# Transfers of an attention and FFN kernel entered in one list, paced by TensorE's columns, with reads of turned weights ahead of writes

## The chip, the cores and the metric

The kernel runs on one core of one Trainium2 chip. A core has TensorE (PE; its weight loads are PEld in the profile), VectorE (DVE), ScalarE (ACT), GpSimd (POOL) and SyncE (SP). In this kernel SP issues nearly every transfer (DMA); 16 DMA engines carry them. The metric is device time in microseconds of one execution.

## The reference, cut to what matters

Attention with a threshold, for 8 batches of 8 heads of 576 rows by 64, and then a bilinear FFN on 4608 rows of 512. All is float32.

```python
scores = scale * np.matmul(q, k.transpose(0, 1, 3, 2))
thresh = np.max(scores, axis=-1, keepdims=True) - tau
scores = np.where(scores >= thresh, scores, -1000000000.0)
attn = np.exp(scores - np.max(scores, axis=-1, keepdims=True))
attn = attn / (np.sum(attn, axis=-1, keepdims=True) + 1e-09)
x = bridge(np.matmul(attn, v))        # (B,H,S,D) -> (B*S, H*D)
return (x @ w_a) * (x @ w_b) @ w_out  # d_model 512, d_ff 1536
```

## The kernel before

Two heads are handled together, a pair; there are 32 pairs, four to a batch. A pair's 576 query rows are cut into four units of 128 rows and a tail of 64 (u = 0 to 3 and NT = 4), which makes 160 units. The main loop has one slot for each unit, and three more (PV_LAG). A slot g does the first steps of unit g and later steps of the units before it, and fills TensorE's time with pieces of the FFN of rows already finished. The order of work on every engine, SP included, is the order in which the loop writes it: `keep_order` ties each instruction to the one before it on its engine. TensorE's order is planned in columns: `advance` draws matmuls of the FFN from a generator until the columns owed in this slot are used up.

The path of a unit:

- Slot g: TensorE computes its scores (L352), 576 columns of them; VectorE takes the maxima (L359); ScalarE the exponentials into the tile `tw` (L380); VectorE cuts at the threshold and sums (L383), and takes the reciprocal (L396); ScalarE normalises (L402).
- Slot g + 1, `turn_blocks`: VectorE transposes `tw` in blocks of 32 by 32 (L446), and SP writes it to a scratch buffer in DRAM, `swap`, by four transfers of 144 KB (72 KB for a tail; L457). `tw` has three buffers.
- Slot g + 2, `turn_back`: SP reads `swap` back in another order, into the tile `wT` (L466: one transfer of 576 KB; L469: two of 144 KB for a tail). By these two transfers the weights are turned. `wT` has two buffers.
- Slot g + 3, after 65% of the slot's share of FFN work, if the unit ends a part: `weighted` multiplies the weights by v (L483), and ScalarE and VectorE take the product out of PSUM (L490, L491). A part is units 0 and 1, or units 2, 3 and the tail. The first batch has other parts, and its first eight units are turned on TensorE and not through DRAM.

Within a slot SP's order is: the four writes of the unit before (`turn_blocks`), behind VectorE's transposes; then the read of the unit before that (`turn_back`, after `weighted` when there is one in the slot, since it needs the buffer of `wT` that `weighted` frees); at the end the loads of q (L147, three slots ahead of use), of k (L147, four ahead) and of v (L170), and the outputs that were pending when the slot began (`store`, L833). q and k are transposed by VectorE (`prep`, L320) one or two slots ahead of their scores. In a later batch the first eight slots hold units 0 and 1 of its four pairs, the next twelve units 2, 3 and the tail.

The FFN's first two matrices are L633 (products of a fast scheme with seven multiplications, 128 columns each) and L706, the last L763 (256 columns). Its results go through tiles `kept` of the tag `osb` (four buffers, shared with `u`, L663) to the output.

Of the kernel before, what the change touches and what calls it, by code (L numbers as in the profile page):

```python
# [22 lines left out]
PV_LAG = 3  # L23
# [7 lines left out]
ROOM = 1024  # L31
PORTIONS = (0.3, 0.35, 0.15, 0.2)
# [20 lines left out]
def kernel(  # L53
# [69 lines left out]
    scratch = pool("scratch", 3, space=bass.MemoryType.DRAM)  # L123
# [11 lines left out]
    def load(i, name, engine=nc.sync):  # L135

        b, hp = pairs[i]
        src = {"q": q, "k": k}[name[0]]
        n0, n1 = {"k": (0, NB), "q0": (0, HALF // Q), "q1": (HALF // Q, NB)}[name]
        bufs = HP if name == "k" else Q_BUFS  # L140
        most = NB if name == "k" else NB - HALF // Q
        t = work.tile([P, most, Q], FP32, tag=name[0] + "T", bufs=bufs, name=name[0] + "T")[:, 0:n1 - n0]
        for j in range(2):
            rows = src[b, 2 * hp + j].rearrange("(e n) d -> e n d" if name == "k" else "(n e) d -> e n d", e=Q)
            for h in range(2):
                r = slice((2 * j + h) * Q, (2 * j + h + 1) * Q)
                engine.dma_start(t[r], rows[:, n0:n1, h * Q:(h + 1) * Q])  # L147
        loaded.setdefault(i, {})[name] = t
# [9 lines left out]
    def load_v(i, again=False):  # L158
# [3 lines left out]
        for j in range(2):  # L162
            rows, half = v[b, 2 * hp + j], loaded[i]["v"][j * D:(j + 1) * D]
            if i >= HP or again:
                if i < HP:
                    rows = rows.rearrange("(c s p) d -> p c s d", c=2, p=Q)
                else:
                    rows = rows.rearrange("(p c s) d -> p c s d", c=2, p=Q)
                for c in range(2):
                    nc.sync.dma_start(half[c * Q:(c + 1) * Q], rows[:, c])  # L170
            else:
                nc.sync.dma_start(half, rows.rearrange("(s p) d -> p s d", p=D))
# [21 lines left out]
    for F in range(NF):  # L194
# [4 lines left out]
             "layer": False, "reading": False, "first": 0}  # L199
# [117 lines left out]
    def prep(i, name):  # L317

        mT = loaded[i].pop(name).rearrange("p n e -> p (n e)")
# [121 lines left out]
    def turn_blocks(i, u):  # L441
# [10 lines left out]
        for g in range(G):  # L452
            if u < NT:
                to, n = swap[g], G
            else:
                to, n = swap[g % 2, (1 - g // 2) * D:(2 - g // 2) * D], 2
            nc.sync.dma_start(to.rearrange("(r p) e -> p r e", p=Q),  # L457
                              t[g * Q:(g + 1) * Q, 0:n * NSLOT].rearrange("p (r s) e -> p r (s e)", r=n))

    def turn_back(i, u):  # L460

        swap = swaps.pop((i, u)).rearrange("g p e -> p g e")
        if u < NT or i < HP:
            turned[i, u] = turned_tile()
            n = G if u < NT else 2
            nc.sync.dma_start(turned[i, u][:, 0:n].rearrange("p g s e -> p g (s e)"), swap)  # L466
        else:
            for y in range(2):
                nc.sync.dma_start(turned[i, 2 + y][:, G].rearrange("p s e -> p (s e)"), swap[:, y])  # L469
# [69 lines left out]
    def weighted(i, h):  # L539

        b, hp = pairs[i]
        n = width(i, h)
# [287 lines left out]
    def store(n):  # L830

        for _ in range(n):
            nc.sync.dma_start(*pending.pop(0))  # L833
# [7 lines left out]
    running = {"ffn": None, "owed": 0.0, "left": 0, "done": 0, "rest": 0, "room": 0}  # L841

    def advance(cols):
        running["owed"] += cols
        while running["owed"] > 0:
# [19 lines left out]
            else:  # L865
                running["owed"] -= step
                running["left"] -= step
                running["done"] = running["done"] + step if rest else 0
# [56 lines left out]
    for g in range(len(units) + PV_LAG):  # L925
        written = len(pending)
        state["converted"] = state["added"]
        here = g < len(units)
        converting = bool(early.get(g)) or bool(early.get(g - 1))
        if here:  # L930
            i, u = units[g]
            scores(i, u)
        exchange_blocks()
# [33 lines left out]
        if g > BY_PE:  # L967
            advance(PORTIONS[1] * pace)
            n = g - PV_LAG
            if BY_PE <= n < len(units) and part(*units[n]):  # L970
# [4 lines left out]
                weighted(*part(*units[n]))  # L975
                running["owed"] -= NSLOT * width(*part(*units[n])) // 2
            if BY_PE + 1 < g <= len(units) + 1:
# [43 lines left out]
    state["over"] = True  # L1021
    while complete or blocks or running["ffn"] is not None:
# [35 lines left out]
```

## Time and profile before

| what | us |
|---|---|
| median of 3 runs | 1463.66 (1454.89 to 1464.56) |
| the profiled execution | 1467.37 |
| its span, first to last instruction | 1465.6 |
| TensorE busy | 1387.9 |
| VectorE busy | 1014.9 |
| ScalarE busy | 682.9 |
| GpSimd busy | 479.5 |

The granted clock of TensorE was 0.994 of full speed on average. The transfers moved 223.21 MB, 152 GB/s over the span; packets of the queue on which SP issues took 60.7% of the time of the 16 DMA engines.

In the profile's lines the letter L is followed by the line in the kernel; "out<-in" names what an instruction writes and reads. SPq stands for SP's queue, whose instructions only issue transfers and wait. A row of waits gives who waited, for whom, the sum in us, how many times, and the longest. "Issue" as a releaser means that the engine waited for nothing that the profile shows. A row of issued transfers ends in the size of one and the median time from issue to landing. A line of a timeline starts with the start in us, and how long. [...]

### The profile page before, as it was taken

The numbers are of one execution on the slowest core, as the hardware profiler recorded it, in microseconds if no ns is written. First come the engines' busy times: TensorE is split into PE (matmuls) and PEld (weight loads), VectorE is DVE, ScalarE is ACT, GpSimd is POOL, SyncE is SP. The second block draws the span as 40 slices with busy tenths as digits, with TensorE's granted clock in tenths as the row PEclk, the third lists the DMA queues.
The fourth block names the chain that finished last, engine by engine and source line by source line (L and its number), as shares of the span: only waits on it lengthen the run. The fifth ranks groups of instructions, "written<-read, shape, count | busy, mean of one in ns | idle before, by whom it ended". The sixth has DMA issues, their size and how long they took to land.

```text
span 1465.6 us, 76332 instructions
## 1 busy us (share of the span) xinstructions
PE 1387.9 (95%) x34208; PEld 1248.2 (85%) x34208; DVE 1014.9 (69%) x2245; ACT 682.9 (47%) x1243; POOL 479.5 (33%) x668
## 2 busy tenths in 40 slices
PE   5788999999999999999999899999999999999998
PEld 4677687987989889899998788998898979989997
DVE  6898688787767787586757677767767776755223
ACT  5787455545545554454444445444545455431110
POOL 2774713423060606033334224150606060605000
PEclk9999999999999999999999999999999999999999
DMA  9976677668756775577555766477656776450000
GB/s 217 227 207 181 155 183 190 167 169 189 195 135 160 165 203 145 137 174 180 142 135 138 163 165 169 121 177 167 173 147 144 179 188 165 122 148 30 4 17 17
DMA packets 325080, 223.21 MB, mean 152 GB/s; under 512 B 169616, under 2 KB 308880, under 8 KB 324752
## 3 DMA queue, kind: packets, MB, share of 16 engines
q1 hardware_dynamic: 322384, 217.73, 60.7%
q8 instruction: 269, 4.41, 1.3%
q10 hardware_dynamic: 2368, 0.59, 0.2%
q14 instruction: 59, 0.48, 0.1%
HBM read 128.58 MB, written 89.65 MB: 149 GB/s over the span
## 4 chain that ended last, share of the span: by engine, by line
PE 78%; DVE 7%; DMA 5%; SPq 5%; issue 3%; ACT 1%; POOL 1%; ACTq 0%; DVEq 0%; POOLq 0%
PE pab L633 24%; PE pab L706 18%; PE po L763 17%; PE pv L483 9%; PE sc L352 9%; DMA wT<-swap 2%; SPq L457 2%; DVE mx L359 2%; SPq L147 1%; DMA qT<-in_q_dram 1%; DVE tw L446 1%; DVE tw L383 1%; PE po L809 1%; SPq L225 1%; POOL kept L732 0%
## 5 line engine op out<-in xcount | busy, mean ns | idle before, releaser
L402 ACT ACTIVATE tw<-tw,rcp 128x576 f32<-128x576 f32 x272 | 197.8, 769 | 216.9 <-DVE rcp L396 216.8
L359 DVE TENSOR_REDUCE mx<-sc 128x1 f32<-128x576 f32 x288 | 205.6, 751 | 134.6 <-PE sc L352 131.3
L380 ACT ACTIVATE tw<-sc,bias,scalars 128x576 f32<-128x576 f32 x288 | 239.3, 831 | 9.8 <-DMA vm<-in_v_dram 0.2
L599 POOL TENSOR_TENSOR h<-h,u 128x512 f32<-128x512 f32 x28 | 35.1, 1272 | 621.8 <-DVE h L676 485.8
L383 DVE SCALAR_TENSOR_TENSOR tw<-sc,thr,tw 128x576 f32<-128x576 f32 x288 | 223.0, 798 | 14.0 <-ACT tw L380 13.8
L763 PE MATMUL po<-wo_sb,h 64*64 64x256 f32 x3264 | 222.9, 377 | 0.0
L352 PE MATMUL sc<-kT,qT 64*64 64x288 f32 x2016 | 192.0, 405 | 10.5 <-ACT xt L490 4.7
L446 DVE STREAM_TRANSPOSE tw<-tw 128x576 f32<-128x576 f32 x272 | 196.0, 754 | 0.8 <-ACT tw L402 0.8
L483 PE MATMUL pv<-wT,vm 64*64 64x160 f32 (+3 forms) x5184 | 182.4, 275 | 14.3 <-DMA wT<-swap 8.0
L763 PEld LDWEIGHTS po<-wo_sb,h 64*64 64x64 f32 x3264 | 167.4, 133 | 24.9
L483 PEld LDWEIGHTS pv<-wT,vm 64*64 64x64 f32 x5184 | 166.2, 135 | 25.3 <-issue 10.4
L763 PE MATMUL po<-sums_u,h 64*64 64x256 f32 x2448 | 163.9, 376 | 1.6 <-DVE h L714 1.6
L732 POOL TENSOR_TENSOR h<-h 128x256 f32<-128x256 f32 x168 | 117.4, 728 | 114.6 <-PE po L763 100.5
L352 PEld LDWEIGHTS sc<-kT,qT 64*64 64x64 f32 x2016 | 115.1, 133 | 32.5 <-ACT xt L490 12.3
L763 PEld LDWEIGHTS po<-sums_u,h 64*64 64x64 f32 x2448 | 123.4, 133 | 20.7 <-DVE h L714 2.3
L633 PE MATMUL pab<-xU,wb_sb 64*64 64x128 f32 x4096 | 133.5, 270 | 0.2 <-issue 0.2
L379 ACT ACTIVATE bias<-mx,scalars 128x1 f32<-128x1 f32 x288 | 83.0, 288 | 100.6 <-DVE mx L359 100.5
L633 PEld LDWEIGHTS pab<-xU,wb_sb 64*64 64x64 f32 x4096 | 127.6, 133 | 2.6 <-issue 0.5
L491 DVE COPY xT<-pv 64x128 f32<-64x128 f32 (+1 forms) x136 | 38.1, 280 | 120.3 <-PE pv L483 119.1
L633 PE MATMUL pab<-xS,wa_sb 64*64 64x128 f32 x2048 | 110.8, 270 | 3.2 <-POOL xS L506 2.0
L490 ACT COPY xT<-pv 128x128 f32<-128x128 f32 (+1 forms) x68 | 17.6, 258 | 206.0 <-PE pv L483 205.9
L706 PE MATMUL pab<-xS,wb_sb 64*64 64x256 f32 (+1 forms) x1536 | 99.9, 359 | 2.9 <-issue 2.9
(137 smaller groups left out, 2429.0 us busy)
## 6 DMA issues: line engine op xcount, KB each, us to landing
swap<-tw SPq DMA_DIRECT2D x480, 144.0 KB, 2.6
wT<-swap SPq DMA_DIRECT2D x120, 576.0 KB, 4.7
vm<-in_v_dram SPq DMA_DIRECT2D x128, 72.0 KB, 3.3
swap<-tw SPq DMA_DIRECT2D x128, 72.0 KB, 2.0
kT<-in_k_dram SPq DMA_DIRECT2D x112, 72.0 KB, 4.3
wT<-swap SPq DMA_DIRECT2D x56, 144.0 KB, 2.9
out_dram<-kept SPq DMA_DIRECT2D x30, 256.0 KB, 4.0
qT<-in_q_dram SPq DMA_DIRECT2D x112, 40.0 KB, 4.5
```

Of the source, the lines that this page charges most:

```text
L352: nc.tensor.matmul(sc[j if u < NT else 0][to, c], qT[r, q0:q0 + D], kT[r, c * SH:(c + 1) * SH], start=True, stop=True)
L359: nc.vector.tensor_reduce(mx[:, c], sc[j], axis=AX.XY, op=ALU.max)
L379: nc.scalar.activation(bias[:, j:j + 1], mx[:, j:j + 1], AF.Copy, scale=e_nscale)
L380: nc.scalar.activation(wb[j], sb[j], AF.Exp, bias=bias[:, j:j + 1], scale=e_scale)
L383: nc.vector.scalar_tensor_tensor(out=wv, in0=sb[j], scalar=thr[:, j:j + 1], in1=wv, op0=ALU.is_ge, op1=ALU.mult, accum_out=sums[:, j:j + 1])
L402: nc.scalar.activation(w, w, AF.Copy, scale=rcp[:, j:j + 1])
L446: nc.vector.transpose(w, w)
L483: nc.tensor.matmul(pv[c * D:(c + 1) * D, y], vm[rows, s], wT[y](rows, s), start=(s == 0), stop=(s == NSLOT - 1))
L633: nc.tensor.matmul(out[c * D:(c + 1) * D, r, f * P:(f + 1) * P], w[g][k][rows, w0:w0 + D], moving[k][rows], start=(fresh and k == 0 and f ...
L706: nc.tensor.matmul(pab[c * D:(c + 1) * D, r], w[rows, f // n, k, fs + c * D:fs + (c + 1) * D], moving, start=(k == 0), stop=(k == H - 1))
L732: (nc.vector if state["over"] else nc.gpsimd).tensor_tensor(*a, **kw)
L763: nc.tensor.matmul(po[c * D:(c + 1) * D, r, y], ht[rows, t0:t0 + D], other[rows, f], start=(f == 0), stop=(f == NF // 2 - 1))
```

## The change

From slot 13 on (`state["paced"]`), transfers are no longer issued where the loop asks for them. `post` puts them into a list, `bulk`, with a key and the number of the slot. `pump` takes the oldest entry and issues it; the entry's first transfer also waits for the matmul that stands last in TensorE's order at that place. `passed` counts TensorE's columns as they are written, for scores, FFN and products with v, and calls `pump` once in 320 columns while the list holds something. `flush` empties the list up to given keys where data is about to be used: before a transpose of q or k, before a read of turned weights (its writes), before a product. At a slot's start, entries of the slot before the last are issued, and those of the part whose product the slot holds.

An entry is one write to `swap`, one read, two transfers of q, one of k, two of v, or one output (128 or 256 KB). Reads of `wT` are cut into pieces of 144 KB, one for each of the four blocks of columns. In a slot without a product the read (`turn_back`) is entered at the slot's start, ahead of the slot's writes; in a slot with one it stays behind the product. The scratch buffers are five for each shape, were three. Loads of the FFN's weights stay outside of the list.

```diff
--- before.py
+++ after.py
@@ -29,6 +29,7 @@
 CATCH_UP = 0.05
 PACE_EARLY = 0.04
 ROOM = 1024
+PUMP = 320
 PORTIONS = (0.3, 0.35, 0.15, 0.2)
 RAWS = 4
 TW_BUFS = 3
@@ -120,7 +121,7 @@
     loads = pool("loads", 3)
     work = pool("work", 2)
     small = pool("small", 2)
-    scratch = pool("scratch", 3, space=bass.MemoryType.DRAM)
+    scratch = pool("scratch", 5, space=bass.MemoryType.DRAM)
     psum = pool("psum", 4, space=PSUM)
 
     def banks(n, name):
@@ -132,7 +133,41 @@
     NPR = len(pairs)
     loaded = {}
 
-    def load(i, name, engine=nc.sync):
+    bulk = []
+
+    def post(key, *moves):
+
+        if not state["paced"]:
+            for move in moves:
+                nc.sync.dma_start(*move)
+        else:
+            bulk.append((key, state["slot"], moves))
+
+    def pump(count=1):
+
+        for _ in range(min(count, len(bulk))):
+            behind = next(x.name for x in reversed(nc.cur_bb.bb.instructions) if x.engine == mybir.EngineType.PE)
+            for n, move in enumerate(bulk.pop(0)[2]):
+                moved = nc.sync.dma_start(*move)
+                if n == 0:
+                    tc.add_manual_dep(
+                        moved.ins, behind,
+                        mybir.DependencyInfo(mybir.DependencyClass.Sync, mybir.DependencyReason.DATA),
+                        reason="pace")
+
+    def flush(*keys):
+
+        while any(key in keys for key, _, _ in bulk):
+            pump()
+
+    def passed(columns):
+
+        running["pump"] = running["pump"] + columns if bulk else 0
+        while running["pump"] >= PUMP:
+            running["pump"] -= PUMP
+            pump()
+
+    def load(i, name):
 
         b, hp = pairs[i]
         src = {"q": q, "k": k}[name[0]]
@@ -142,9 +177,9 @@
         t = work.tile([P, most, Q], FP32, tag=name[0] + "T", bufs=bufs, name=name[0] + "T")[:, 0:n1 - n0]
         for j in range(2):
             rows = src[b, 2 * hp + j].rearrange("(e n) d -> e n d" if name == "k" else "(n e) d -> e n d", e=Q)
-            for h in range(2):
-                r = slice((2 * j + h) * Q, (2 * j + h + 1) * Q)
-                engine.dma_start(t[r], rows[:, n0:n1, h * Q:(h + 1) * Q])
+            moves = [(t[(2 * j + h) * Q:(2 * j + h + 1) * Q], rows[:, n0:n1, h * Q:(h + 1) * Q]) for h in range(2)]
+            for some in ([moves] if name != "k" else [moves[0:1], moves[1:2]]):
+                post((name, i), *some)
         loaded.setdefault(i, {})[name] = t
 
     def load_rows(i, name, room, engine=nc.sync):
@@ -166,8 +201,7 @@
                     rows = rows.rearrange("(c s p) d -> p c s d", c=2, p=Q)
                 else:
                     rows = rows.rearrange("(p c s) d -> p c s d", c=2, p=Q)
-                for c in range(2):
-                    nc.sync.dma_start(half[c * Q:(c + 1) * Q], rows[:, c])
+                post(("v", i), *((half[c * Q:(c + 1) * Q], rows[:, c]) for c in range(2)))
             else:
                 nc.sync.dma_start(half, rows.rearrange("(s p) d -> p s d", p=D))
 
@@ -196,7 +230,7 @@
     NPIECES = len(pieces)
     raws, stages, extra, taken = {}, {}, [], {}
     state = {"loaded": 0, "added": 0, "converted": 0, "rows": 0, "sums": False, "through": 0, "over": False,
-             "layer": False, "reading": False, "first": 0}
+             "layer": False, "paced": False, "slot": 0, "reading": False, "first": 0}
 
 
     NSUM = NF // 2 * 3 * CH
@@ -316,6 +350,7 @@
 
     def prep(i, name):
 
+        flush((name, i))
         mT = loaded[i].pop(name).rearrange("p n e -> p (n e)")
         nc.vector.transpose(mT, mT)
         prepared.setdefault(i, {})[name] = mT
@@ -454,19 +489,22 @@
                 to, n = swap[g], G
             else:
                 to, n = swap[g % 2, (1 - g // 2) * D:(2 - g // 2) * D], 2
-            nc.sync.dma_start(to.rearrange("(r p) e -> p r e", p=Q),
-                              t[g * Q:(g + 1) * Q, 0:n * NSLOT].rearrange("p (r s) e -> p r (s e)", r=n))
+            post(("tw", i, u), (to.rearrange("(r p) e -> p r e", p=Q),
+                                t[g * Q:(g + 1) * Q, 0:n * NSLOT].rearrange("p (r s) e -> p r (s e)", r=n)))
 
     def turn_back(i, u):
 
+        flush(("tw", i, u))
         swap = swaps.pop((i, u)).rearrange("g p e -> p g e")
+        key = "wT", i, min(u // 2, 1) if i >= HP else u // 2
         if u < NT or i < HP:
             turned[i, u] = turned_tile()
             n = G if u < NT else 2
-            nc.sync.dma_start(turned[i, u][:, 0:n].rearrange("p g s e -> p g (s e)"), swap)
+            for y in range(0, n, 1):
+                post(key, (turned[i, u][:, y:y + 1].rearrange("p g s e -> p g (s e)"), swap[:, y:y + 1]))
         else:
             for y in range(2):
-                nc.sync.dma_start(turned[i, 2 + y][:, G].rearrange("p s e -> p (s e)"), swap[:, y])
+                post(key, (turned[i, 2 + y][:, G].rearrange("p s e -> p (s e)"), swap[:, y]))
 
     def join(out, lo, hi):
         nc.scalar.copy(out, lo)
@@ -539,6 +577,7 @@
     def weighted(i, h):
 
         b, hp = pairs[i]
+        flush(("v", i), ("wT", i, h))
         n = width(i, h)
         if h < 2:
             groups = G + (n > HALF)
@@ -830,7 +869,7 @@
     def store(n):
 
         for _ in range(n):
-            nc.sync.dma_start(*pending.pop(0))
+            post("out", pending.pop(0))
 
     BLOCK_COLS = NF * 2 * HP * HALF + 2 * NF * DM
 
@@ -838,7 +877,7 @@
 
         return BLOCK_COLS - (NF // 2 * CH if state["sums"] else 0) - (SEVENS * 2 * HP * P if state["first"] >= 3 * SEVENS else 0)
 
-    running = {"ffn": None, "owed": 0.0, "left": 0, "done": 0, "rest": 0, "room": 0}
+    running = {"ffn": None, "owed": 0.0, "left": 0, "done": 0, "rest": 0, "room": 0, "pump": 0}
 
     def advance(cols):
         running["owed"] += cols
@@ -865,6 +904,7 @@
             else:
                 running["owed"] -= step
                 running["left"] -= step
+                passed(step)
                 running["done"] = running["done"] + step if rest else 0
                 running["rest"] = rest
                 running["room"] = min(ROOM, whole // 2)
@@ -924,12 +964,24 @@
         n += size
     for g in range(len(units) + PV_LAG):
         written = len(pending)
+        state["slot"], state["paced"] = g, g > BY_PE + HP
+        while bulk and bulk[0][1] < g - 1:
+            pump()
+        if g - PV_LAG > 0 and g - PV_LAG < len(units) and part(*units[g - PV_LAG]):
+            flush(("wT", *part(*units[g - PV_LAG])))
         state["converted"] = state["added"]
         here = g < len(units)
         converting = bool(early.get(g)) or bool(early.get(g - 1))
+        back = ()
+        if BY_PE + 1 < g <= len(units) + 1:
+            n = g - PV_LAG
+            back = (1 if BY_PE <= n and part(*units[n]) else 0,)
+            if not back[0]:
+                turn_back(*units[g - 2])
         if here:
             i, u = units[g]
             scores(i, u)
+            passed(S)
         exchange_blocks()
         pace = (PACE if g > BY_PE else PACE_EARLY) * BLOCK_COLS
         if g > BY_PE:
@@ -973,8 +1025,9 @@
                     make_x(2 if h == 1 and p >= HP and pairs[p][0] % GT == 0 else 1)
                 make_room()
                 weighted(*part(*units[n]))
+                passed(NSLOT * width(*part(*units[n])) // 2)
                 running["owed"] -= NSLOT * width(*part(*units[n])) // 2
-            if BY_PE + 1 < g <= len(units) + 1:
+            if back and back[0] > 0:
                 turn_back(*units[g - 2])
         for n in early.get(g, [])[:1]:
             convert_first(n)
@@ -1019,6 +1072,8 @@
             first_sums(state["first"] % 3, state["first"] // 3)
             state["first"] += 1
     state["over"] = True
+    pump(len(bulk))
+    state["paced"] = False
     while complete or blocks or running["ffn"] is not None:
         advance(DM)
         store(len(pending))
```

## The prediction

> **What bounds the kernel now.** I read the page first, then TensorE's waits in the stretch that the change can reach, then SP's queue, then the windows.
>
> ```profile
> span 1465.6 us, 76332 instructions
> PE 1387.9 (95%) x34208; PEld 1248.2 (85%) x34208; DVE 1014.9 (69%) x2245; ACT 682.9 (47%) x1243; POOL 479.5 (33%) x668
> swap<-tw SPq DMA_DIRECT2D x480, 144.0 KB, 2.6
> wT<-swap SPq DMA_DIRECT2D x120, 576.0 KB, 4.7
> wT<-swap SPq DMA_DIRECT2D x56, 144.0 KB, 2.9
> ```
>
> TensorE is busy 95% of the span, and neither kernel touches its order of work, nor VectorE's, ScalarE's or GpSimd's. So the change can only move TensorE's idle time. Slots up to 12 post nothing to the list, and after slot 162 the list is empty: the reach is about 128 to 1310 us. The windows give it:
>
> ```profile
> 128.00:1310.00 1182.00, 1144.76 (x28064) 1030.11 (x28060) 857.58 (x1915) 577.39 (x1035) 390.91 (x552) 1.00 0.66 162
> ```
>
> TensorE idles 1182 - 1144.8 = 37.2 us there. Who ended it (us in total, times, longest):
>
> ```profile
> PE pv L483 <- DMA wT<-swap: 8.0, 6, 2.7
> PE pab L633 <- issue: 7.8, 14, 1.9
> PE sc L352 <- ACT xt L490: 4.7, 4, 1.2
> PE sc L352 <- DVE xt L491: 3.2, 3, 1.1
> PE pv L483 <- issue: 2.6, 4, 1.0
> PE sc L352 <- issue: 0.5, 2, 0.3
> ```
>
> Only the first row is a wait for data that a transfer brings. Most rows left out, and the two on xt, are waits for another engine's copies (PSUM banks coming free), which the list does not touch. "Issue" (7.8 + 2.6 + 0.5 = 10.9 us) is TensorE out of instructions: the packet records have a queue of 16 KB instruction packets (q8), and nearly all of these stalls end 1.0 to 1.7 us after such a packet has landed. Ceiling of any gain: 8.0 + 10.9 = 19 us, about 25 with the 0.24 to 0.32 us by which each stall exceeds its idle time (the last matmul's modelled end).
>
> Now SP, the queue that is rearranged, around the longest of the six stalls:
>
> ```profile
> 815.35 2.13 SPq L147 DMA_DIRECT2D qT<-in_q_dram  x4
> 817.52 3.05 SPq L170 DMA_DIRECT2D vm<-in_v_dram  x4
> 820.68 1.19 SPq L833 DMA_DIRECT2D out_dram<-kept  x2
> 821.97 3.06 SPq L457 DMA_DIRECT2D swap<-tw  x4
> 825.13 0.39 SPq L466 DMA_DIRECT2D wT<-swap  x1
> 825.56 3.00 SPq L147 DMA_DIRECT2D kT<-in_k_dram  x4
> 828.67 1.95 SPq L833 DMA_DIRECT2D out_dram<-kept  x2
> 830.73 2.01 SPq L457 DMA_DIRECT2D swap<-tw  x4
> 832.78 1.21 SPq L469 DMA_DIRECT2D wT<-swap  x2
> ```
>
> and TensorE's line at that place:
>
> ```profile
> 836.97 1.46 PE L483 MATMUL pv<-wT,vm 64*64 64x160 f32 x14 [2.68 <-DMA wT<-swap]
> ```
>
> SP runs without a pause, one transfer each 0.45 to 0.75 us. The read at 832.78 belongs to the slot whose scores were reduced from 822.38: SP is a slot behind, and the products wait 2.68 us. So the stalls on wT are stalls on SP's length of queue, not on bandwidth. Where there is no such backlog SP itself idles: 311.9 us in 103 waits for VectorE's transposes (L446), with the read of wT queued behind.
>
> **The change, step by step.** Per pair of heads (five slots, some 40 us).
>
> *Reads at the front of a slot.* Today a read stands behind its slot's four writes, which wait for the transposes and then take 1.8 to 3.1 us to issue. At the front it passes them. Of the six stalls (idle 1.11, 1.08, 1.93, 0.16, 1.01, 2.68 us) the first five are smaller than 2 us, and I count them as gone: 5.3 us. At 832.78 the read passes four writes (2.0 us), but three more pieces of the read before it now stand ahead (3 x 0.45 = 1.4 us): I count half, 1.3 us. With 0.24 us more for each of five: **-7.8 us**. Where the products close a part in the same slot, the read stays behind them as now; it is wanted over a slot later.
>
> *Reads in pieces.* 120 reads of 576 KB become 480 of 144 KB: 360 more issues. L469's row is the same piece: median 0.45 us to issue, 2.9 us to land, against 0.38 and 4.7. The pieces come 320 columns apart. Scores are 576 columns in 16 matmuls of 288 (60 ns apart when dense), so a column is 1.67 ns and a piece comes each 0.53 us: the last lands 3 x 0.53 + 2.9 = 4.5 us after the first is issued, as the whole did. No gain, no loss by itself.
>
> The Trainium skill, "DMA: Bandwidth & Descriptors" (Rules for kernel authors) says to merge small transfers into a large one; its fit for GpSimd-issued ones (2.0 us + bytes over 436 GB/s) would give, as an estimate, 3.4 us for the whole and 4 x 2.3 us for pieces in a row, 6 us worse a read. The rows speak otherwise: pieces overlap, four writes issue within 1.8 us and land 2.6 us each.
>
> *Pacing.* A slot of 7.0 to 8.5 us has 4200 to 5100 columns, 13 to 16 turns. Entries per pair: 20 writes, 18 pieces, q 4, k 4, v 2, about 1 output = 49, 9.8 a slot. The list empties each slot. SP's wait for TensorE costs TensorE nothing: sixteen dense matmuls around one that updates a semaphore take 863 ns, as without. Delayed are the loads: k was issued at a slot's end and is now within the next 2 to 4 us, with its transposes (L320) over a slot off; v has four slots; outputs about half a slot later, with L663 and L472 waiting for their room some three slots on. Price now 0; if SP falls behind, see the second rival. Queued behind a paced transfer are only other transfers, all of the list's order.
>
> *Instruction packets.* From the records: a packet starts 0.66 us after it can first be asked for when no transfer is in flight, 1.6 to 2.0 us with two to six (the earliest place of asking is my reckoning); a fit gives +0.7 us for an output in flight, +0.24 for a write to swap, +0.06 for a read of wT. So cutting the reads does little; spreading outputs and writes helps somewhat. Bounds: nothing lost or gained at one end, all 10.9 gone at the other; more in flight for longer could also cost as much. I take a quarter, **-2.7 us**, near the fit's low price for what is cut.
>
> The skill's "Runtime: NRT & Kernel Launch" (Instruction fetch mechanics) calls refilling mostly hidden; by it this term is 0. The issue rows show otherwise.
>
> *SP's load.* Priced in the rival; in the likely case **+1 us**.
>
> Sum: -7.8 - 2.7 + 1 = -9.5 us. The profiled execution took 1467.4 us (span 1465.6), so 1457.9; the median of the runs shown is 3.7 lower, 1463.7, and the same step from it gives **1454 us**.
>
> **Rivals.**
>
> *SP becomes the bound (slower).* Place: the eight slots of each later batch with units 0 and 1, where q, k and v are loaded too: seven stretches of about 61, 61, 63, 71, 71, 64 and 64 us (179-240, 325-385, 480-543, 641-713, 816-887, 987-1051, 1151-1214). After the change each has 32 writes, 32 pieces, 12 k, 16 q, 12 v = 104 transfers (80 now). Unblocked (0.45, 0.63, 0.46, 0.42 us, 0.045 between): 53.5 us, fits. At the prices of the rows shown (0.55, 0.75, 0.53, 0.76: the wait for one of eight completion counters to come free is in them) 66.5, and with a separate wait instruction for the pace (17 ns and a gap, 0.06 us) 72.7. Over the seven 7 x 72.7 - 455 = 54 us; each stretch has some 5 us of slack before products or transposes wait, 35 in all, so **+19 us**, and without the gain above: 1483. It decides from 0.58 us a transfer (61 / 104). For it: DMA share 0.71 to 0.82 in these stretches, SP already without pause. Against: smaller reads free their counters sooner, and reads use the time in which SP waits for transposes.
>
> *Nothing moves.* The read passes the writes but stands behind loads posted a slot before, and the pace gives back what the place won: wT stalls stay, 1463 (1457 to 1468). For it: the case at 832.78, where net 0.6 us is sure. Against: the five small ones.
>
> *The list calms the transfers.* All wT and issue stalls go: -19 to -25 us, 1440. For it: issue stalls follow packets that start late. Against: the fit.
>
> **How the numbers follow.** Forecast 0.42 (1446 to 1460), calm 0.15 (1436 to 1446), nothing 0.23, SP-bound 0.20 (1470 to 1500). A measurement of this kernel tells about 1%, 14.6 us, from no change: faster takes the calm case and most of the forecast's lower half (0.17), 0.32; slower nearly all of the SP case, 0.19; the rest 0.49. Range: 1438 cuts off some of the calm case, 1480 half of the SP case.
>
> **What would show it.** Right: the row pv L483 <- DMA wT under 2 us; reads of wT in pieces that SP issues before its slot's writes, landing in about 3 us; SP's waits now mostly for TensorE; issue rows 6 to 11 us. Wrong: pv waiting for wT over 8 us in the seven stretches with SP without pause (second rival); new waits of L320 for a load, or of L380 for a write to swap (tw not free); or issue rows that go to near 0 or double.

## The result, and the profile after

The changed kernel takes 1464.78 us (median of 22 runs, 1458.36 to 1472.92), the kernel before 1463.56 (22 runs, 1454.89 to 1469.02). The ratio is 1.0011, with a 95% interval of 0.9993 to 1.0029: no change, where 1454 was forecast. The profiled execution of the changed kernel took 1464.33 us.

The lines of the new page that answer to those shown of before:

```profile
span 1462.5 us, 77884 instructions
PE 1389.9 (95%) x34208; PEld 1266.7 (87%) x34208; DVE 1016.2 (69%) x2245; ACT 682.6 (47%) x1243; POOL 479.4 (33%) x668
...
wT<-swap SPq DMA_DIRECT2D x544, 144.0 KB, 2.9
swap<-tw SPq DMA_DIRECT2D x480, 144.0 KB, 2.9
```

The change does what it says: all reads of turned weights are pieces now (544 for 120 + 56), and no engine computes more or less than before. (In these counts a matmul stands as two records: 2016 of the scores' line are 1008 matmuls of the loop.) Next, the window from 128 to 1310 us of the changed kernel (busy time and count of PE, PEld, DVE, ACT, POOL, then clock, DMA share and GB/s):

```profile
128.00:1310.00 1182.00, 1148.68 (x28188) 1046.37 (x28184) 861.18 (x1925) 579.65 (x1041) 391.58 (x553) 1.00 0.63 163
```

TensorE idles 1182 - 1148.7 = 33.3 us there, 3.9 less than before. Who ended that idle time in the changed kernel (us in total, times, longest):

```profile
PE pv L521 <- DMA wT<-swap: 10.5, 8, 2.8
PE sc L387 <- ACT xt L528: 7.0, 6, 1.2
...
PE pv L521 <- issue: 1.9, 2, 1.1
...
PE pab L672 <- issue: 1.0, 3, 0.5
...
PE sc L387 <- issue: 0.2, 1, 0.2
```

The two rows that the forecast was about went the opposite way to each other. The wait for turned weights, which was to fall to 1.4 us (8.0 - 5.3 - 1.3), rose from 8.0 to 10.5. TensorE's want of instructions, which was to lose a quarter, fell from 10.9 to 3.1. A second profile of the unchanged kernel (below) gave 5.8 and 11.7, so about 2 us of such a sum is chance; the second fall is far beyond that.

SP's queue of the changed kernel around the place of the longest stall:

```profile
817.96 2.05 SPq L151 DMA_DIRECT2D wT<-swap  x4
820.12 2.43 SPq L151 DMA_DIRECT2D qT<-in_q_dram  x4
822.64 2.49 SPq L151 DMA_DIRECT2D vm<-in_v_dram  x4
825.25 1.48 SPq L151 DMA_DIRECT2D out_dram<-kept  x2
826.83 2.69 SPq L151 DMA_DIRECT2D wT<-swap  x4
829.62 1.81 SPq L151 DMA_DIRECT2D swap<-tw  x4
831.53 3.71 SPq L151 DMA_DIRECT2D kT<-in_k_dram  x4
835.35 1.21 SPq L151 DMA_DIRECT2D out_dram<-kept  x2
836.65 1.04 SPq L151 DMA_DIRECT2D wT<-swap  x2
```

and TensorE's line there:

```profile
839.11 2.36 PE L521 MATMUL pv<-wT,vm 64*64 64x160 f32 x26 [2.78 <-DMA wT<-swap]
```

The read at 836.65 does stand ahead of its slot's writes now. But the loads of k and the outputs of the slot before stand ahead of it. Its slot's scores were reduced from 824.36, so it is issued 12.3 us after its slot's start; before it was 832.78 - 822.38 = 10.4 us. The stall is as long as it was: 2.78 for 2.68 us.

How full SP is says why an entry that is late stays late. "Blocked" is here the sum of the gaps between SP's instructions and of the wait instructions that last over 0.15 us, taken from SP's records in the window; the rest of the time SP issues or goes through short wait instructions.

| 128 to 1310 us | before | after |
|---|---|---|
| transfers issued | 1241 | 1596 |
| wait instructions of their own | 333 | 1293 |
| blocked, us | 433 | 224 |
| blocked in the seven stretches of units 0 and 1, 455 us in all | 92 | 18 |

In those stretches SP has hardly a pause left: one transfer each (455 - 18) / 716 = 0.61 us. Whatever holds an entry back there isn't made up before the stretch ends.

### The profile page after: what moved, and what is told of

It is laid out like the page before. It is cut to its first block, busy times and chain, and to the rows that moved or that the text cites. A ratio compares the mean times of both kernels' runs of the same rounds, so it can differ in the third digit from the quotient of the medians.

```text
span 1462.5 us, 77884 instructions
## 1 busy us (share of the span) xinstructions
PE 1389.9 (95%) x34208; PEld 1266.7 (87%) x34208; DVE 1016.2 (69%) x2245; ACT 682.6 (47%) x1243; POOL 479.4 (33%) x668
## 4 chain that ended last, share of the span: by engine, by line
PE 85%; DVE 6%; DMA 3%; issue 2%; ACT 1%; POOL 1%; SPq 0%; DVEq 0%; POOLq 0%; ACTq 0%
PE pab L672 27%; PE po L802 19%; PE pab L745 18%; PE sc L387 10%; PE pv L521 10%; DMA wT<-swap 2%; PE po L848 1%; DVE mx L394 1%; DVE tw L418 1%; POOL kept L771 1%; DVE tw L481 1%; DMA swap<-tw 1%; PE tp L462 1%; DVE low L294 0%; DMA scalars<-in_tau_dram 0%
## 5 line engine op out<-in xcount | busy, mean ns | idle before, releaser
L638 POOL TENSOR_TENSOR h<-h,u 128x512 f32<-128x512 f32 x28 | 35.1, 1272 | 615.7 <-DVE h L715 475.5
L521 PE MATMUL pv<-wT,vm 64*64 64x160 f32 (+3 forms) x5184 | 186.0, 278 | 18.6 <-DMA wT<-swap 10.5
L521 PEld LDWEIGHTS pv<-wT,vm 64*64 64x64 f32 x5184 | 169.7, 137 | 29.2 <-issue 20.7
L802 PEld LDWEIGHTS po<-wo_sb,h 64*64 64x64 f32 x3264 | 172.5, 133 | 20.0
L387 PEld LDWEIGHTS sc<-kT,qT 64*64 64x64 f32 x2016 | 117.8, 133 | 31.1 <-ACT xt L528 12.2
L802 PEld LDWEIGHTS po<-sums_u,h 64*64 64x64 f32 x2448 | 127.8, 133 | 16.4 <-DVE h L753 2.3
```

The lines of the kernel that those rows point to most:

```text
L387: nc.tensor.matmul(sc[j if u < NT else 0][to, c], qT[r, q0:q0 + D], kT[r, c * SH:(c + 1) * SH], start=True, stop=True)
L521: nc.tensor.matmul(pv[c * D:(c + 1) * D, y], vm[rows, s], wT[y](rows, s), start=(s == 0), stop=(s == NSLOT - 1))
L802: nc.tensor.matmul(po[c * D:(c + 1) * D, r, y], ht[rows, t0:t0 + D], other[rows, f], start=(f == 0), stop=(f == NF // 2 - 1))
```

## The experiments

The kernels of a group (e1 to e4, e5 to e8, e9 and e10, e11 and e12) ran on one chip, and each is compared with runs of the kernel before on that chip. "wT" is the sum of TensorE's waits for turned weights, "issue" the sum of its rows of issue, both between 128 and 1310 us of one profiled execution. A difference of two ratios in the table is uncertain by some 0.003, which is 4 us.

| kernel | ratio to before, 95% | wT, us | issue, us |
|---|---|---|---|
| before | 1 | 8.0 (again: 5.8) | 10.9 (again: 11.7) |
| the change | 1.0011 [0.9993, 1.0029] | 10.5 | 3.1 |
| place alone (e1_front) | 0.9994 [0.9967, 1.0020] | 0.4 | 14.5 |
| pieces alone (e11_pieces) | 1.0109 [1.0085, 1.0133] | 14.9 (19.4, see there) | 7.2 (2.7) |
| place and pieces, no list (e2_nolist) | 0.9947 [0.9926, 0.9967] | 7.0 | 2.3 |
| the change, reads whole (e3_whole) | 1.0055 [1.0036, 1.0074] | 2.2 | 15.3 |
| the change, no wait for TensorE (e8_nowait) | 0.9951 [0.9936, 0.9967] | 5.0 | 3.6 |
| the change, wait on an older matmul (e10_old) | 0.9971 [0.9951, 0.9991] | 6.5 | 4.9 |
| the change, an entry in 80 columns (e7_pump80) | 1.0007 [0.9989, 1.0026] | 13.6 | 2.9 |
| e2_nolist, reads in halves (e6_half) | 0.9979 [0.9964, 0.9994] | 0.2 | 10.7 |
| the change, reads at the list's head (e4_head) | 1.0074 [1.0047, 1.0100] | 8.8 | 2.6 |
| e8_nowait, reads at the list's head (e9_nowait_head) | 1.0000 [0.9979, 1.0021] | 4.1 | 4.4 |
| e2_nolist, k and v loaded by ScalarE's queue (e5_act) | 1.0537 [1.0511, 1.0562] | 1.0 | 11.8 |

Single profiles scatter: the profiled executions of e11_pieces and e4_head are 9 and 7 us under their medians, so their rows are rather too small; those of e10_old and e3_whole are 5 and 4 us under, that of e6_half 5 over.

### The place alone

The kernel before, with the read entered ahead of the slot's scores and writes where the slot holds no product; reads stay whole, SP's order is the only thing that differs.

```diff
         here = g < len(units)
...
+        ahead = False
+        if BY_PE + 1 < g <= len(units) + 1:
+            n = g - PV_LAG
+            ahead = not (BY_PE <= n and part(*units[n]))
+            if ahead:
+                turn_back(*units[g - 2])
...
-            if BY_PE + 1 < g <= len(units) + 1:
+            if BY_PE + 1 < g <= len(units) + 1 and not ahead:
                 turn_back(*units[g - 2])
```

> The kernel before with one part of the change alone: reads of turned weights issued at the front of a slot, whole, with no list and no pace. Theory A (place in SP's queue decides the stalls on wT, and pieces or pace decide the stalls on instructions): stalls of the products on wT fall from 8 us to under 3, stalls on issue stay at 9 to 13 us; time 1455 to 1460. Rival B (TensorE's idle time only changes its name; whatever goes comes back elsewhere): 1461 to 1467 with another row grown by as much. Rival C (SP's length of queue is the bound): as A for wT, since SP issues no more than before.

Measured: 0.9994. TensorE's waits in this kernel, the rows on wT and the two largest on issue:

```profile
PE pab L633 <- issue: 11.9, 15, 2.3
...
PE pv L483 <- issue: 1.3, 3, 0.8
...
PE pv L483 <- DMA wT<-swap: 0.4, 1, 0.4
```

The place does what it was priced for: one stall on wT is left, of 0.4 us. The read that ends a part is first issued 1.6 us after its slot's start (median of 55) for 5.5 before. Yet the time stays, within about 4 us either way: issue rose from 10.9 to 14.5, and TensorE's idle time in the window fell only from 37.2 to 35.1 us (busy 1146.9).

### Place and pieces, without the list

The changed kernel with the list switched off, so that each transfer is issued where the loop asks for it.

```diff
-        state["slot"], state["paced"] = g, g > BY_PE + HP
+        state["slot"], state["paced"] = g, False
```

> The changed kernel without list and pace: reads at the front of a slot and in pieces of 144 KB, everything issued where the loop asks for it. Theory A: wT as in the front run plus what three more issues a read cost; if the pieces are what calms the instruction packets, issue stalls are near 3 us and time 1450 to 1456; if the pace is, they are back at 9 to 13 us and time 1457 to 1464. Rival B: 1461 to 1467. Rival C: 360 more issues with no pace make SP later, wT stalls over 10 us, time 1465 to 1475.

Measured: 0.9947, faster than both the kernel before and the changed one; with the list without the wait (below) the best of these versions. TensorE's waits in it:

```profile
PE pv L521 <- DMA wT<-swap: 7.0, 6, 1.8
...
PE pab L672 <- issue: 1.3, 3, 0.6
...
PE pv L521 <- issue: 0.8, 1, 0.8
```

So the list with its pace costs 1.0011 - 0.9947 = 0.0064 of the time, 9 us. And cutting the reads, with the place, gains 0.9994 - 0.9947 = 0.0047, 7 us (the pair differs in the scratch buffers too, five and three, but no row of SP's waits in the kernel with three is a write waiting for a read); the issue rows fell by 12.2 us against the place alone, and wT gave 6.6 of these back.

### The change with whole reads

```diff
-            for y in range(0, n, 1):
-                post(key, (turned[i, u][:, y:y + 1].rearrange("p g s e -> p g (s e)"), swap[:, y:y + 1]))
+            post(key, (turned[i, u][:, 0:n].rearrange("p g s e -> p g (s e)"), swap))
```

> The changed kernel with the reads of wT whole (576 KB in one entry), list and pace kept. Theory A: with three entries fewer before it, a read at a part's end comes 1 to 2 us earlier, wT stalls 5 to 8 us against 10.5; issue stalls 3 us if the pace calms the packets, 9 us or more if the pieces do; time 1458 to 1463. Rival B: 1462 to 1467. Rival C: SP has 360 issues fewer, wT stalls under 4 us and time under 1457.

Measured: 1.0055. The waits, in the changed kernel with whole reads:

```profile
PE pab L671 <- issue: 9.2, 12, 1.8
...
PE pv L520 <- DMA wT<-swap: 2.2, 2, 1.4
```

Against the place alone the list and its pace cost 1.0055 - 0.9994 = 0.0061: the same 9 us as with pieces, so this price doesn't hang on the cutting. How it comes about here stays open, though; the list without the wait was run only with pieces. The reads that end a part land 0.6 us before their product's slot starts (median; place alone 1.7 us), SP is blocked 90 us in the seven stretches, wT is only 1.8 us more than with the place alone and issue 0.8. The profiled executions differ by 5.5 of the 9 us, and the rest was not found. And the issue rows are back at 15.3: it is the size of the reads, not their spacing, that sets them.

### Pieces alone

The kernel before, its read still behind the writes, in four pieces.

```diff
-            nc.sync.dma_start(turned[i, u][:, 0:n].rearrange("p g s e -> p g (s e)"), swap)
+            for y in range(n):
+                nc.sync.dma_start(turned[i, u][:, y:y + 1].rearrange("p g s e -> p g (s e)"), swap[:, y:y + 1])
```

> The kernel before with one part alone: reads of wT in pieces of 144 KB, issued where they were, behind the slot's writes, with no list. If pieces are worth what the two pairs of runs say (-0.47% without the list, -0.44% with it) and the front is worth little (-0.06%): issue stalls 2 to 4 us, 1455 to 1459, as with the front. If the front is what keeps pieces from making reads late: wT stalls over 12 us, at least two stretches of half clock, 1461 to 1470.

Measured: 1.0109, slower by 16 us. The waits:

```profile
PE pv L484 <- DMA wT<-swap: 14.9, 12, 3.0
...
PE pv L484 <- issue: 5.3, 2, 4.5
...
PE pab L634 <- issue: 1.3, 2, 1.0
```

Behind the writes, four issues instead of one come at the worst place: the read lands 3.3 us (median) after the start of its product's slot, before it was 2.7. SP is blocked 24 us in the seven stretches, before 92. The longest row of issue is no want of instructions:

```profile
836.25 1.04 SPq L470 DMA_DIRECT2D wT<-swap  x2
```

```profile
839.43 2.03 PE L484 MATMUL pv<-wT,vm 64*64 64x160 f32 x29 [4.46 <-issue]
```

The two pieces landed at 839.24 and 839.61, and no instruction packet landed between 832.83 and the stall's end. So I count its 4.5 us as a wait for turned weights: wT 19.4, issue 2.7. Together the rows account for a part of the 16 us only (wT 11.4 more, issue 8.2 less, in an execution that was 9 us under the median); the rest was not found. The rows of FFN on issue still shrink, from 7.8 to 1.3. Place and pieces are thus no sum: -0.06% and +1.09% alone, -0.53% together. The pieces win instructions and need the place to pay for SP's time.

### The list without the wait

The changed kernel, list and order kept, but no entry waits for TensorE.

```diff
-                if n == 0:
+                if False:
                     tc.add_manual_dep(
```

> The changed kernel with its list and the order of entries kept, but without the wait of an entry for TensorE's matmul. Theory F: SP issues as soon as it comes to an entry, reads land as without a list, 1455 to 1459. Rival G: as theory F. If the order alone costs (entries stand later in SP's order than where the loop asks for them, behind other entries' own waits), 1462 to 1467.

Measured: 0.9951, with these waits of TensorE:

```profile
PE pv L521 <- DMA wT<-swap: 5.0, 7, 1.4
...
PE pab L672 <- issue: 1.5, 3, 0.9
...
PE pv L521 <- issue: 1.4, 2, 0.8
```

It is as fast as without a list: the order costs nothing that these runs can tell, and the wait costs all of the 9 us. Not because the wait's instructions fill SP: it is blocked 224 us with them and 215 without; they take some 45 us more of the rest, and the transfers' own issues 53 us less. What differs is where it may go. The profile's account of SP's waits in the changed kernel, the first five rows:

```profile
SPq L151 <- PE pab L672: 173.7, 241, 6.6
SPq L151 <- DVE tw L481: 96.5, 36, 6.4
SPq L151 <- PE po L802: 76.4, 168, 2.3
SPq L151 <- PE pab L745: 67.2, 146, 1.9
SPq L151 <- PE sc L387: 65.7, 62, 4.8
```

Four of the five are the pace. With it SP may not run ahead of TensorE's place, even where data and room are there; reads that end a part are issued 5.1 us after their slot's start, without the wait 3.9, and land 2.0 against 0.7 us after the start of their product's slot (medians).

For the matmuls that the window held in the kernel before, the profiled executions took 1177.7 us with the wait and 1167.1 without. Of these 10.6 us, 5.5 are waits on wT, and 5.1 come from three stretches in which TensorE's clock was granted at half, against none (last section); issue is 0.5 us less. At full clock TensorE is busy with them for 1139 us in both, so the wait doesn't slow the matmuls themselves.

### The wait on an older matmul, and a denser list

Two kernels that loosen the pace in different ways: each entry waits for the matmul 120 places before the last one, or an entry is taken in 80 columns instead of 320.

```diff
-            behind = next(x.name for x in reversed(nc.cur_bb.bb.instructions) if x.engine == mybir.EngineType.PE)
+            PES = [x.name for x in nc.cur_bb.bb.instructions if x.engine == mybir.EngineType.PE]
+            behind = PES[-1 - OLD]
```

> The changed kernel with each entry waiting for a matmul 120 places earlier in TensorE's order (more than a slot's worth) instead of the last one: the wait is nearly always over when SP comes to it, and its instruction stays. Theory G (the wait's instruction is what costs SP, some 73 us of its time in 950 more instructions): SP busy as in the changed kernel, wT stalls 8 us or more, 1461 to 1467. Theory F (being held back to TensorE's place costs): as without the wait, wT 5 us, 1454 to 1458.

```diff
-PUMP = 320
+PUMP = 80
```

> The changed kernel with a turn of the list each 80 columns instead of 320. Theory F (the list costs by holding entries back in TensorE's time, which pushes SP's whole queue later): entries go out at once, reads land as early as without a list, wT stalls 6 to 8 us, time 1455 to 1459. Rival G (the list costs by its additional waits on SP, one for each entry, whatever the distance): as the changed kernel, 1462 to 1467.

Measured: 0.9971 with the older matmul, 1.0007 with the denser list. The first gives back 0.0040 of the 0.0060 that the wait costs (the intervals are 0.002 wide to either side, so the share is rough). The second gives nothing back; its row of TensorE's waits on wT:

```profile
PE pv L521 <- DMA wT<-swap: 13.6, 10, 2.9
```

So the price is not in the spacing of the entries but in SP's being tied to the very matmul that TensorE has reached. The number of SP's wait instructions doesn't set it either. In the window there are 343 without the wait and 1293 with it; the older matmul leaves 571, so they did not stay, as had been expected, and the denser list leaves 692. It has lost 601 of the 950 additional ones and is no faster.

### Reads at the head of the list

Since the read at 836.65 stood behind older loads, two kernels put reads of wT at the list's head: one with the wait, one without it.

```diff
-            bulk.append((key, state["slot"], moves))
+            at = len(bulk)
+            if key[0] == "wT":
+                at = next((n for n, x in enumerate(bulk) if x[0][0] != "wT"), len(bulk))
+            bulk.insert(at, (key, state["slot"], moves))
...
-        while bulk and bulk[0][1] < g - 1:
+        while any(x[1] < g - 1 for x in bulk):
```

> The changed kernel with reads of wT entered at the head of the list, ahead of loads and outputs of the slot before. Theory A: the eight stalls on wT (10.5 us in the changed kernel) go but for 0 to 3 us, issue stalls stay near 3 us: 1452 to 1458. Rival B: 1461 to 1467, other rows take over. Rival C: the loads that the reads pass come late in turn, a wait of VectorE's transposes of q and k (L358) or of a product for v appears, 1462 or more.

> The list without its wait for TensorE, and with reads of wT entered at the head of the list, ahead of loads of the slot before. If it is the place in SP's order that decides once SP has time to spare (it idles 214 us of 1182 without the waits, 139 with them): the stalls on wT go from 5.0 us to under 2, issue stalls 2 to 4, time 1450 to 1455. If SP's work alone decides, as in the run with reads at the head and the wait: wT 5 to 7 us, time 1455 to 1458. If loads of q and k come late in turn: 1458 or more, with a wait of scores on a transposed q or k.

Measured: 1.0074 and 1.0000, 0.006 and 0.005 worse than the same with reads in their turn. TensorE's waits of the first, two of its rows:

```profile
PE sc L390 <- DVE xt L532: 5.5, 2, 3.0
...
PE sc L390 <- DMA kT<-in_k_dram: 1.3, 1, 1.3
```

and, of the second, a row of SP's waits and one of VectorE's:

```profile
SPq L154 <- DMA swap<-tw: 34.1, 25, 2.4
```

```profile
DVE kT L358 <- DMA kT<-in_k_dram: 11.1, 5, 2.8
```

At the head a read meets its own writes before they have landed, and SP, which works in order, stands: 34.1 us in 25 waits, against 3.4 in 3 without the move. And what was overtaken is late in its turn: VectorE waits for k, and TensorE for VectorE. The wT stalls of the first kernel fell only from 10.5 to 8.8. Over the matmuls of the window, TensorE's waits that are neither on wT nor on issue rose from 19.4 to 28.9 us with the wait and from 19.1 to 26.2 without it, which is most of the 7 to 9 us in the time. (In the second expectation SP's 139 us leave out the time inside wait instructions; with it they are the 224 above.)

### Loads on another queue

To unload SP, k and v are issued by ScalarE; otherwise place and pieces without a list.

```diff
-                post((name, i), *some)
+                post((name, i), *some, engine=nc.scalar if name == "k" else nc.sync)
...
-                post(("v", i), *((half[c * Q:(c + 1) * Q], rows[:, c]) for c in range(2)))
+                post(("v", i), *((half[c * Q:(c + 1) * Q], rows[:, c]) for c in range(2)), engine=nc.scalar)
```

> The run without list (reads in front, pieces), with the loads of k and v issued from ScalarE's queue instead of SP's: the same transfers, eight in five slots fewer on SP. Theory D (pieces calm the instruction packets, worth some 10 us; the 360 more issues make SP late, and the lateness is what brings the stalls on wT back): stalls on wT fall from 7.0 us to under 2, issue stalls stay at 1 to 4 us, time 1447 to 1453 unless ScalarE loses by issuing. Rival E (the stalls on wT come from slower landing of many transfers, not from SP's queue): wT stays at 6 to 8 us, time as the run without list, 1456.

Measured: 1.0537, 77 us slower. A row of ScalarE's waits, and one of TensorE's:

```profile
ACT bias L414 <- DMA kT<-in_k_dram: 48.6, 11, 7.3
```

```profile
PE sc L387 <- DVE tw L418: 19.5, 14, 4.3
```

Each waiting transfer holds up ScalarE's exponentials behind it, and through VectorE the scores. SP could carry these waits because nothing but transfers is queued on it. That the wT row is 1.0 here says little: with TensorE late, the reads have more time. The granted clock averages 0.978 over its runs, before 0.994, which by the busy time of 1390 us makes some 22 of the 77 us (last section). Of its 11.8 us on issue, 7.0 are four stalls that end 2.3 to 8.0 us after an instruction packet landed, the others 1.1 to 1.6 us after one; so 4.8 are left that look like a want of instructions.

### Reads in halves

The kernel without the list, its reads of 576 KB in two pieces instead of four.

```diff
-            for y in range(0, n, 1):
-                post(key, (turned[i, u][:, y:y + 1].rearrange("p g s e -> p g (s e)"), swap[:, y:y + 1]))
+            for y in range(0, n, 2):
+                post(key, (turned[i, u][:, y:y + 2].rearrange("p g s e -> p g (s e)"), swap[:, y:y + 2]))
```

> The run without list, with reads in two pieces of 288 KB instead of four of 144 KB. Theory D: SP's load and the calm both lie between whole and quarters: stalls on wT 2 to 5 us, issue stalls 4 to 10 us, time 1455 to 1461. Rival E: wT stalls near 7 us still. If the instruction packets only care that no transfer exceeds some size, issue stalls are all or nothing: near 2 or near 14 us.

Measured: 0.9979, between whole and quarter reads, and from whole ones (0.9994) not told apart. The largest row of TensorE's waits on issue:

```profile
PE pab L672 <- issue: 9.2, 15, 1.4
```

With 288 KB there is next to no wait on wT (0.2 us), but the issue rows stay near those of whole reads.

### The kernel before, profiled again

> The kernel before, unchanged, for a second profile: how far its rows move from one execution to the next. The first profile took 1467.4 us, 3.8 over the median. If that was chance in the stalls: wT and issue stalls together 13 to 17 us instead of 18.9 and fewer stretches of half clock, 1460 to 1465. If the rows repeat within 2 us, the difference lies elsewhere (start of the run).

Measured: one execution of 1464.53 us, with these rows:

```profile
PE pab L633 <- issue: 9.8, 15, 1.9
...
PE pv L483 <- DMA wT<-swap: 5.8, 3, 2.6
```

With two smaller rows issue is 11.7 in all. So a fall of wT from 8.0 to 5 could be chance, while 0.4 (place alone) or 14.9 (pieces alone), and issue at 2.3 to 4.9 with pieces against 10.7 to 15.3, hardly are.

### Why cut reads save instructions

The packets of TensorE's instructions (q8) were timed in the same way as for the prediction, from the earliest place where each can be asked for (my reckoning) to its start:

| kernel | mean with a read of wT in flight, us | without | 95% of all start within |
|---|---|---|---|
| place alone, reads of 576 KB | 1.94 | 1.19 | 3.35 |
| the change with whole reads | 1.93 | 1.14 | 3.37 |
| halves, two in flight | 1.72 | 1.20 | 3.49 |
| kernels with pieces of 144 KB | 1.2 to 1.3 | 1.05 | 2.3 to 2.6 |

With a large read in flight an instruction packet starts some 0.75 us later, with small ones 0.2. These sizes hang on the reckoning: with the place of asking taken instead from the earliest start, in instructions, among the twenty packets to either side, they are 0.4 us for the place alone, 0.6 for the change with whole reads, 0.3 for halves and 0 to 0.3 for pieces, and none for the kernel before, where packets without a read in flight are as late. That the size of the reads sets the issue rows is shown by the kernels above; how a read delays a packet is only inferred. The Trainium skill, "DMA: Bandwidth & Descriptors" (Queues, rings and completion order), says that each DMA engine takes turns between its queues and finishes a whole packet of one before it goes to the next. A whole read would put a longer run of descriptors on each engine than a piece does, which would agree in sign with these delays; but taking turns packet by packet doesn't by itself make a longer run hold others up longer, and no run here looked at the packets' bounds.

## Why the prediction was wrong

**What bounds the kernel** held in part: no engine's busy time came down, and TensorE's idle time moved by less than the ceiling of 19 us. But stretches at half clock, which count as busy, moved as well (three for two), and the prediction has no term for them.

**Reads at the front, -7.8 us.** The mechanism was right and the gain was there to be had: with the place alone 0.4 of 8.0 us is left. But it reached the time neither in that kernel, where TensorE waited 3.6 us more for instructions, nor in the change, where the row is 10.5. Of the read at 832.78 I had counted half of the stall as gone; it grew by 0.1.

**Pieces, "no gain, no loss by itself".** This step failed twice over. I priced only when the last piece lands. By themselves the pieces cost 16 us, with reads that land later where SP has no time to spare (+11.4 us on wT); with the place they gain 7 us, through instructions.

**Pacing, "price now 0".** This is the step that turned the sum: it costs 9 us, with whole reads (0.0061) as with pieces (0.0064). I had asked whether SP's wait costs TensorE anything and whether the list empties within a slot, and not what it costs that SP may no longer run ahead in stretches where it has no pause to catch up in. For pieces the runs show that (reads issued 1.2 us later, wT 5.5 us more, three more stretches of half clock in the profiled pair); for whole reads, where SP has pauses, it is shown only that list and wait together cost as much, and not by which path.

**Instruction packets, -2.7 us.** Right in kind, mis-sized: it measured 10.9 - 3.1 = 7.8. The fit had given +0.06 us for a read of wT in flight; the same fit on the kernel with the place alone gives +0.37, with whole reads in the list +0.44. In the trace of before reads are mostly in flight together with writes and loads, so that the fit could not tell whose delay it was. The quarter, near the low end of the bounds, was a guess where the trace could give no number.

**SP's load, +1 us, and the rival in which SP becomes the bound.** Over the window an issue takes (1182 - 224) / 1596 = 0.60 us, over the 0.58 from which I said it decides, and the pauses in the seven stretches went from 92 to 18 us, as that rival foretold. Its +19 us did not come by itself: without the wait SP is as full there (25 us of pauses) and the kernel is at 0.9951. A full SP is not yet a late one.

**The sum by what was measured**: place -0.06%, pieces on top of it -0.47%, list and pace +0.64%, together +0.11%. The rival that nothing moves came nearest, and for the reason given there: the read passes the writes but stands behind loads posted a slot before, and the pace gives back what the place won. Only that it is a balance of -8 and +9 us, and no standstill, wasn't in it. What I named as signs: SP's waits are for TensorE, as said; issue is under the 6 to 11 foreseen; pv's wait for wT is over the 2 us that would have borne out the forecast. The second rival's sign came too, without its price: 8.8 of the 10.5 us on wT fall in the seven stretches, with SP nearly without pause.

How the pace's 9 us divide could be shown in part. In the one profiled pair they are 5.5 us of wT and 5.1 of half clock. Over all timed runs the clock has a smaller share: the granted clock averages 0.9926 against 0.9942 without the wait, which is 0.0016 x 1390 = 2.2 us of TensorE's time (see below). With wT at 5.5 us, some 1 us would then be left, which is within what the runs can tell.

## What to carry to other kernels

An in-order queue that issues transfers should be let run ahead as far as data and room allow; tying it to the engine that it serves had a price here, 9 us, even though the wait itself is free for that engine. Look at what large transfers do to the fetching of instructions: cutting reads of 576 KB to 144 KB paid here, but only with an earlier place for them. And a fit on a trace in which two causes mostly come together gives a price for neither.

## What the runs showed of the hardware that I had not expected

A stall of TensorE can cost more than its own length. The windows around the long stall of the kernel before, and around one of the changed kernel (us of the window, busy time and count of PE, PEld, DVE, ACT, POOL, then the granted clock, DMA share and GB/s):

```profile
833.70:837.10 3.40, 0.72 (x12) 0.29 (x5) 1.65 (x5) 0.44 (x1) 0.00 (x0) 1.00 0.66 167
837.10:840.50 3.40, 3.40 (x50) 3.21 (x53) 0.00 (x0) 0.00 (x0) 0.00 (x0) 0.50 0.61 152
```

```profile
340.60:344.00 3.40, 0.85 (x16) 0.39 (x8) 2.45 (x7) 1.30 (x4) 2.49 (x4) 1.00 0.77 176
344.00:347.40 3.40, 3.40 (x49) 3.32 (x53) 0.70 (x2) 0.00 (x0) 3.08 (x7) 0.51 0.76 170
347.40:350.80 3.40, 3.40 (x104) 3.25 (x101) 2.12 (x8) 1.16 (x4) 2.49 (x6) 0.99 0.71 170
```

After a wait of 2.7 or 2.55 us the clock is granted at half for 3.41 us, in which 50 and 49 records of matmuls start where the next 3.4 us have 104: another 1.7 us lost, which no row of waits shows, since TensorE counts as busy. Between 128 and 1310 us there were two such stretches in the kernel before and three in the changed one. The length of a wait alone doesn't decide. Waits of 1.91, 2.55, 2.68 and 2.78 us in these two kernels were followed by one, and so were two of 0.97 and 0.87 us with 0.4 us of work between them (at 394.9), and single ones of 1.39 us (reads at the list's head) and 1.51 us (the same without the wait). But waits of 1.93 us in the kernel before, of 2.97 us with pieces alone, and of 2.63 us in the second profile of the kernel before were not; the windows around the last:

```profile
252.40:255.80 3.40, 0.77 (x12) 0.27 (x5) 3.36 (x6) 1.39 (x3) 2.40 (x4) 1.00 0.70 210
255.80:259.20 3.40, 3.40 (x104) 3.20 (x107) 1.88 (x8) 0.38 (x2) 3.10 (x6) 1.00 0.77 180
```

The Trainium skill, "TensorE: Matmul & The Clock Gate" (HAM oscillation), gives as its rule that there be no idle gaps of over about 3.4 us. The half-speed stretch has that length here; but no single wait of TensorE between 128 and 1310 us of these two kernels was longer than 2.8 us, so that shorter gaps can be enough. What decides between waits of the same length was not found.
